# Staggering the two row halves of the PV matmuls, and a later first score step

## The chip, the cores and the metric

The kernel runs on one core of a Trainium2 chip. Times are device microseconds (us) of one execution. The engines have short names in the profile: PE is TensorE (matmuls), PEld its weight loads, DVE is VectorE, ACT is ScalarE, POOL is GpSimd, SP is SyncE, which here only issues DMAs. ACTq and SPq are the DMA-issuing instructions of ACT and SP.

## What is computed

A transformer block of which attention and feed-forward part work on the same normalised input: 2048 tokens of 576 features, 32 heads of 18 features each, a sliding window of 256 tokens, and a gated feed-forward layer with 4608 hidden features. All in bfloat16.

```python
def _A_ref(x, wqkv, wo):
    B, S, D = x.shape
    H = 32; Dh = D // H; W = 256
    q, k, v = split_into_heads(x @ wqkv)
    scores = jnp.einsum("bhqd,bhkd->bhqk", q, k) * (Dh ** -0.5)
    mask = (idx[:, None] - idx[None, :] >= 0) & (idx[:, None] - idx[None, :] < W)
    p = _softmax(jnp.where(mask[None, None], scores, -1e9), axis=-1)
    o = jnp.einsum("bhqk,bhkd->bhqd", p, v)
    return merge_heads(o) @ wo

def _B_ref(x, w1, w3, w2):
    h = _silu(jnp.einsum("bsd,df->bsf", x, w1)) * jnp.einsum("bsd,df->bsf", x, w3)
    return jnp.einsum("bsf,fd->bsd", h, w2)

xn = _layernorm(x)
return x + _A_ref(xn, A_wqkv, A_wo) + _B_ref(xn, B_w1, B_w3, B_w2)
```

## The kernel before

The 2048 tokens are worked in four chunks of 512 (`c` = 0 to 3). Each chunk has three phases on TensorE: the projections to q, k and v (line 437), gate/up (line 668), and the down projection with the output projection of attention (lines 719 and 725). The program is written as one list of operations (`add`); each goes to its engine in the order of the list, and `resolve` (line 90) puts in the semaphore waits that the buffers' readers and writers call for. An engine, ACT's and SP's DMA issues included, takes its instructions in this order, so one that waits holds those behind it.

**Gate/up** runs in 36 units (`u`). A unit is 9 pairs of matmuls (`unit_pairs`), each pair one matmul on the array's rows 0 to 63 and one on rows 64 to 127, both with 512 moving columns, into two PSUM banks, gate and up. Then `unit_tanh` (ACT, line 677) and two products in `unit_h` (DVE, lines 683 and 686) make 128 rows of `hT`. Three pairs of banks (`JOBS`) are taken in turn by units and by PV calls; two more (`SC`) belong to the scores.

**Attention** is put in between the units. The heads are worked in 8 groups of 4 (`G`), and a group's 512 queries in `NS` score steps (4 in the first chunk, 5 later; `steps_of`, line 547). A score step (`score_step`, line 882) is two to three pairs of matmuls into the two `SC` banks (line 561), one exp on ACT that reads both banks and writes a `pt` slot (line 570), and masks on POOL (line 597). The next score step can write the banks only when that exp is done.

When score steps come is planned by a clock that counts pairs of matmuls (`clock`; a slot in the text is one pair of gate/up). The first step comes when the clock reaches `start` (line 860): 20 in the first chunk, 46 in the others. After each step `spaced_step` (line 893) spreads the steps that are left over the room up to slot `last`, at least 7.5 slots apart, and a step that falls due within three slots after a unit's last pair is taken ahead of that pair.

At the end of units 2 and 3 of the first chunk, `span_main(2, G, "act", ...)` (line 965) issues DMAs that copy q and k of head groups 2 to 7 from `stage` into the layout of the scores: the two for q at unit 2, from ACT's queue (line 502 in `span_issue`), the three for k at unit 3, from SP's. `span_last` (line 967) sends further ones from SP at units 4 and 5. Groups 0 and 1 were copied before gate/up.

**PV** (`pv`, line 600) multiplies the exponentials with v, and there are four calls in each chunk, each for two head groups: three behind a unit of gate/up, at least `PV_AFTER` = 20 slots after their last score step, and the fourth in the down projection (line 995). A call goes through the key blocks of all score steps. For each key block it issues a wave of eight matmuls: two groups (`gi`), two pairs of heads (`pr`), and two row halves (`p`) of 64 keys each. Each matmul takes a 64 x 32 tile of the array (20 columns used): row half `p` and column strip `q = 2 * gi + pr`. All eight matmuls of a wave have the same number of moving columns, `nb * KB`, with `KB` = 64. Row half `p` adds up in its own bank, `banks[p]`. The key blocks of a call have, in units of 64 columns, widths 5, 3, 5, 2, 1, 5, 2, 5, 2 in the first chunk and 5, 3, 5, 3, 5, 2, 1, 5, 2, 1, 4, 4 in the others. The results are turned by DVE (`pv_out`, line 627), scaled, turned again and copied to `oT`, which the output projection reads at the end of the chunk.

The order before, in the loops of lines 610 to 614: wave by wave, in a wave strip by strip, and in a strip row half 0 and then row half 1.

Of the kernel before, what the change touches and what calls it, by code (L numbers as in the profile page):

```python
# [44 lines left out]
class _Prog:  # L45
# [13 lines left out]
    def add(self, eng, fn, r=(), w=(), j=(), dma=None, after=()):  # L59
        deps = []  # L60
        for k in r:
            deps += self.bufs[k].writers
        for k in w:
            g = self.bufs.get(k)
            if g is not None:
                deps += g.ahead(eng)
        for k in j:
            g = self.bufs[k].before
            if g is not None:
                deps += g.ahead(eng)  # L70
        op = _Op(eng, fn, deps + list(after), dma)
        op.after = tuple(after)
        self.n[eng] += 1
        op.pos = self.n[eng]
        if dma is not None:
            self.dma_count[dma] = self.dma_count.get(dma, 0) + 16
            op.cnt = self.dma_count[dma]
        for k in r:
            self.bufs[k].readers.append(op)
        for k in w:  # L80
            self.bufs[k] = _Gen([op], self.bufs.get(k))
        for k in j:
            self.bufs[k].writers.append(op)
        for k in w:
            if self.bufs[k].before is not None:
                self.bufs[k].before.before = None
        self.ops.append(op)
        return op
# [76 lines left out]
def bass_parallel_sum__sliding_block__glu_gated_swiglu__prompt_kernel(  # L165
# [24 lines left out]
    VW = 20  # L190
# [5 lines left out]
    add = P.add  # L196

    with ExitStack() as es:

        def sb(name, shape, dtype=dt.bfloat16):  # L200
            return es.enter_context(nc.sbuf_tensor(name, shape, dtype))

        NXP, NOF, NPT, NW13, NW2, NOD = 7, 4, 10, 3, 4, 2
        KB, NB, NV = 64, CH // 64, 12
# [20 lines left out]
        va = sb("va", [128, NV, G, 2, VW])  # L225
# [5 lines left out]
        def pt_slot(sl):  # L231
            kind, n = sl
            if kind == "pt":
                return pt[:, n, :, :]
            if kind == "sh":
                two = stage[:, 2 * n:2 * n + 2, :]
            else:
                two = hT[:, NF - 8 + 2 * n:NF - 6 + 2 * n, :]
            return two.rearrange("p t c -> p (t c)").rearrange("p (q r) -> p q r", r=2)

        def pt_keys(sl):
            kind, n = sl
            if kind == "pt":
                return [("pt", n)]
            if kind == "sh":
                return [("sh", 2 * n), ("sh", 2 * n + 1)]
            return [("h", NF - 8 + 2 * n), ("h", NF - 7 + 2 * n)]
# [16 lines left out]
        PS = es.enter_context(nc.psum_tensor("ps", [128, 8, 512], dt.float32))  # L264
# [6 lines left out]
        def ring():  # L271
            nonlocal ring_ctr
            i = ring_of[ring_ctr % 4]
            ring_ctr += 1
            return i

        def job():
            nonlocal job_ctr
            i = job_ctr % 3
            job_ctr += 1  # L280
            return JOBS[i]
# [263 lines left out]
        pt_of = {}  # L545

        def steps_of(c):

            if c == 0:
                return [[(0, 0, 5), (5, 5, 3)], [(1, 1, 5), (6, 6, 2), (7, 7, 1)],  # L550
                        [(2, 2, 5), (4, 4, 2)], [(3, 3, 5), (4, 6, 2)]]
            return [[(0, 0, 5), (-2, 0, 3)], [(1, 1, 5), (5, 5, 3)], [(2, 2, 5), (-3, 0, 2), (-4, 0, 1)],
                    [(3, 3, 5), (6, 6, 2), (7, 7, 1)], [(-1, 0, 4), (4, 4, 4)]]
# [45 lines left out]

        def pv(c, j, banks):  # L600

            seen = set()
            n_all = sum(len(st) for st in steps_of(c))
            n = 0
            for s, st in enumerate(steps_of(c)):
                col = 0
                for kb, q0, nb in st:
                    n += 1
                    pos = (c * NB + kb) % NV
                    for gi in range(2):  # L610
                        g = 2 * j + gi
                        sl = pt_of[(c, g, s)]
                        for pr in range(2):
                            for p in range(2):
                                first = (p, gi, pr) not in seen
                                seen.add((p, gi, pr))
                                q = 2 * gi + pr
                                add("pe", lambda e, p=p, q=q, pr=pr, sl=sl, g=g, pos=pos, q0=q0, nb=nb, col=col, first=first, n=n: e.matmul(  # L618
                                    PS[32 * q:32 * q + VW, banks[p], q0 * KB:(q0 + nb) * KB],
                                    va[64 * p:64 * p + 64, pos, g, pr, :],  # L620
                                    pt_slot(sl)[64 * p:64 * p + 64, col * KB:(col + nb) * KB, pr],
                                    start=first, stop=(n == n_all), tile_position=(64 * p, 32 * q), skip_group_check=True),
                                    r=pt_keys(sl) + [("va", pos)], **{"j" if any(k[0] == p for k in seen - {(p, gi, pr)}) or not first else "w": [("ps", banks[p])]})
                    col += nb

        def pv_out(b, i):
            add("dve", lambda e: e.transpose(uqs[i], PS[:, b, :]), r=[("ps", b)], w=uq_keys[i])
# [111 lines left out]
        for t in range(2):  # L739
# [3 lines left out]
            w=["wv"], dma="wv")  # L743
# [61 lines left out]
        for h in range(2):  # L805
# [9 lines left out]
            for n, (dst, src) in enumerate(moves):  # L815
                dealt.append(add("pool", lambda e, dst=dst, src=src: e.tensor_copy(dst, src),
                                 r=[f"wqk{h}", "wqkd"], **{"j" if n else "w": [f"wp{h}"]}))
# [32 lines left out]
        for c in range(NC):  # L850
# [6 lines left out]
            total = 9 * NF + len(att) + 3 * PV_COST  # L857
            if c:
                total += 9 * sum(COST[kind] for kind, _ in PROJ)
            start = 20 if c == 0 else 46  # L860
            last = total - 12
            nxt = soon = start
            clock = 0.0
# [55 lines left out]
            for u in range(NF):  # L919
# [18 lines left out]
                if next_pv in pv_ready and clock >= pv_ready[next_pv] and next_pv < 3:  # L938
                    j = next_pv
                    next_pv += 1  # L940
                    banks = job()
                    pv(c, j, banks)
                    clock += PV_COST
                    for g in (2 * j, 2 * j + 1):
                        for s in range(NS):
                            if pt_of[(c, g, s)][0] != "h":
                                free.append(pt_of[(c, g, s)])
                    later(u, lambda b=banks: (pv_out(b[0], 0), pv_out(b[1], 1), o_scale(0)))
                    later(u + 1, lambda j=j: (o_turn(2 * j, 0), o_turn(2 * j, 1), o_scale(1)))
                    later(u + 2, lambda j=j: o_turn(2 * j + 1, 0))  # L950
                    later(u + 3, lambda j=j: (o_turn(2 * j + 1, 1), o_pack(j, "sp")))
# [16 lines left out]
                if c == 0 and u == 13:  # L968
                    for t in range(4):
                        rows = A_wo[252 * (t // 2):252 * (t // 2) + 252, :].rearrange("(s p d) f -> p s d f", p=2, d=Dh)[t % 2, :, :, :]  # L970
                        add("sp", lambda e, t=t, rows=rows: e.dma_start(wo[0:126, t, :], rows),
                            r=["woz"], dma="wo", **{"j" if t else "w": ["wo"]})
# [13 lines left out]
            banks = ()  # L986
            for n, item in enumerate(p2_list(c)):
                p2_item(c, item, xs)
                if n == 3:
                    for u in sorted(side):  # L990
                        for what in side.pop(u):
                            what()
                elif n == 19:
                    banks = (ring(), ring())
                    pv(c, 3, banks)
                    pv_out(banks[0], 0)
                    pv_out(banks[1], 1)
                    o_scale(0)
                    o_turn(6, 0)
                    o_turn(6, 1)  # L1000
                    o_scale(1)
                    o_turn(7, 0)
                    o_turn(7, 1)
                    o_pack(3, "act")
                elif n == 40 and c + 1 < NC:
                    xn_send((c + 1) * TB + 3)
                elif n == 300 and c + 1 < NC:
                    xn_swap(c + 1, ("sp", "sp"))
                elif n in (100, 120) and c + 2 < NC:
                    t = (c + 2) * TB + (n == 120)  # L1010
                    xslot[t] = load_x(t)
# [31 lines left out]
```

## Time and profile before

| | |
|---|---|
| median of 3 runs | 564.29 us (563.03 to 564.5) |
| the profiled execution's own time | 562.96 us |
| its span (first to last instruction) | 561.3 us |
| granted TensorE clock, mean | 1.000 |
| PV matmuls (L618) | 1440 in 16 calls, 4% of the chain that ended last |
| score matmuls (L561) | 720, 6% of that chain |
| exps (L570) | 152, about 1.02 us each for 1024 elements |
| tanh of a unit (L677) | 144, 0.593 us each |

"Line" is the line of the kernel, so L618 is the matmul of PV. A matmul's length in a timeline includes its way through the array (376 ns for 512 columns), and matmuls overlap, so the distance between starts tells the rate. A busy share of 99% does not mean that no time is lost: what stands between one matmul's columns and the next one's start has to be read from the starts. The chain that ended last is followed back from the last instruction, each time to what released it.

### The profile page before, as it was taken

Reading aid. Unit: us, or ns where it says so; the run is one execution under the profiler, and the core shown is the slowest. Engines: PE = TensorE matmul, PEld = TensorE weight load, DVE = VectorE, ACT = ScalarE, POOL = GpSimd, SP = SyncE. Lnnn points to the kernel's source line nnn. Section 1 sums busy time; section 2 is a strip of 40 time slices with the busy share of each in tenths; the row PEclk is TensorE's granted clock in tenths of the full one; section 3 lists DMA queues with packets and bytes.
Section 4 is the critical chain, followed back from the end, with each engine's and each line's share of the span. In section 5 each row is a group of like instructions: output and inputs, shape, how many; then the busy total and the mean of one; then the engine's idle time right before and its main releaser. Section 6 shows DMA issues by size and latency. Waiting matters only on the chain.

```text
span 561.3 us, 15707 instructions
## 1 busy us (share of the span) xinstructions
PE 555.2 (99%) x6765; PEld 330.0 (59%) x6765; DVE 315.9 (56%) x586; ACT 253.3 (45%) x349; POOL 163.9 (29%) x384
## 2 busy tenths in 40 slices
PE   7999999999999999999999999999999999999998
PEld 3544544677655455477755545547776454555776
DVE  7666788710366778851046668884114567767211
ACT  3476666100286766600038677650004676666000
POOL 6433344400033445430003444533000333433000
PEclk9999999999999999999999999999999999999999
DMA  9986969965566477596546655969563674460552
GB/s 246 220 171 159 205 171 202 226 177 158 130 142 139 113 162 157 130 214 179 158 106 139 161 123 126 162 162 205 156 172 69 137 172 123 123 162 12 138 148 64
DMA packets 126565, 85.83 MB, mean 153 GB/s; under 512 B 33976, under 2 KB 124272, under 8 KB 126496
## 3 DMA queue, kind: packets, MB, share of 16 engines
q1 hardware_dynamic: 124469, 82.39, 63.0%
q10 hardware_dynamic: 2024, 2.43, 1.8%
q8 instruction: 53, 0.87, 0.7%
q14 instruction: 19, 0.13, 0.1%
HBM read 71.29 MB, written 2.36 MB: 131 GB/s over the span
## 4 chain that ended last, share of the span: by engine, by line
PE 97%; DMA 1%; DVE 1%; ACT 0%; ACTq 0%; POOL 0%; SPq 0%; issue 0%
PE ps L668 49%; PE ps L719 25%; PE ps L437 9%; PE ps L561 6%; PE ps L618 4%; PE ps L725 3%; DMA xp<-in_A_x_dram 1%; DVE xn L370 0%; ACT hT L570 0%; ACTq L502 0%; DVE stats L358 0%; DVE stats L360 0%; ACT xnT L389 0%; ACT th L677 0%; POOL rstd L364 0%
## 5 line engine op out<-in xcount | busy, mean ns | idle before, releaser
L668 PE MATMUL ps<-xnT,w 64*128 64x512 bf16 x1400 | 180.7, 376 | 0.0
L668 PE MATMUL ps<-xnS,w 64*128 64x512 bf16 x1120 | 151.6, 376 | 0.0
L719 PE MATMUL ps<-w,hT 128*128 128x288 bf16 x1152 | 147.1, 286 | 0.0
L683 DVE SCALAR_TENSOR_TENSOR gs<-th,ps 128x512 bf16<-128x512 bf16 x144 | 98.0, 680 | 79.6 <-ACT th L677 78.8
L570 ACT ACTIVATE pt<-ps 128x1024 bf16<-128x1024 f32 (+1 forms) x112 | 113.2, 1011 | 65.1 <-PE ps L561 64.6
L719 PEld LDWEIGHTS ps<-w,hT 128*128 128x128 bf16 x1152 | 112.1, 98 | 30.3 <-issue 1.7
L597 POOL TENSOR_TENSOR pt<-pt,mk 128x128 int32<-128x128 int32 (+1 forms) x199 | 80.8, 427 | 87.0 <-ACT pt L570 87.0
L686 DVE SCALAR_TENSOR_TENSOR hT<-gs,ps 128x512 bf16<-128x512 bf16 x144 | 98.9, 687 | 4.9
L668 PEld LDWEIGHTS ps<-xnT,w 64*128 64x128 bf16 x1400 | 64.9, 94 | 61.0 <-issue 0.3
L677 ACT ACTIVATE th<-ps 128x512 bf16<-128x512 f32 x144 | 85.4, 593 | 23.1 <-PE ps L668 22.8
L668 PEld LDWEIGHTS ps<-xnS,w 64*128 64x128 bf16 x1120 | 53.7, 94 | 57.0
L732 DVE TENSOR_TENSOR ofin<-ps,xp 128x288 bf16<-128x288 f32 x32 | 14.7, 458 | 119.7 <-PE ps L725 119.7
L450 ACT ACTIVATE stage<-ps 128x512 bf16<-128x512 f32 x16 | 9.6, 597 | 145.6 <-PE ps L437 143.2
L597 POOL TENSOR_TENSOR hT<-hT,mk 128x128 int32<-128x128 int32 (+1 forms) x31 | 12.4, 422 | 162.4 <-ACT hT L570 162.4
L561 PE MATMUL ps<-qv,kv 64*128 64x320 bf16 (+4 forms) x528 | 51.2, 260 | 0.1
L561 PEld LDWEIGHTS ps<-qv,kv 64*128 64x128 bf16 x528 | 25.3, 94 | 28.3 <-ACT pt L570 0.6
L437 PE MATMUL ps<-xnT,wp 64*128 64x512 bf16 (+1 forms) x360 | 38.3, 355 | 0.0
L570 ACT ACTIVATE stage<-ps 128x1024 bf16<-128x1024 f32 x24 | 24.6, 1024 | 12.6 <-PE ps L561 12.6
L640 DVE STREAM_TRANSPOSE od<-oq 128x256 bf16<-128x256 bf16 x64 | 25.8, 427 | 6.3 <-POOL oq L633 6.3
L437 PEld LDWEIGHTS ps<-xnT,wp 64*128 64x128 bf16 x360 | 17.4, 94 | 15.6 <-issue 0.7
L725 PE MATMUL ps<-wo,oT 128*128 128x288 bf16 x160 | 24.8, 286 | 0.0
L633 POOL TENSOR_TENSOR oq<-uq,rden 128x288 bf16<-128x288 f32 x16 | 10.8, 676 | 40.1 <-DVE rden L632 40.1
(58 smaller groups left out, 343.6 us busy)
## 6 DMA issues: line engine op xcount, KB each, us to landing
w<-in_B_w_dram SPq DMA_DIRECT2D x210, 192.0 KB, 4.2
w<-in_B_w_dram SPq DMA_DIRECT2D x72, 288.0 KB, 3.2
xp<-in_A_x_dram SPq DMA_DIRECT2D x28, 144.0 KB, 3.8
out_dram<-ofin SPq DMA_DIRECT2D x32, 72.0 KB, 2.1
xnS<-xnT SPq DMA_DIRECT2D x8, 256.0 KB, 4.8
oT<-od SPq DMA_DIRECT2D x48, 36.0 KB
pt<-in_A_wqkv_dram SPq DMA_DIRECT2D x4, 288.0 KB, 8.2
hT<-in_B_w_dram SPq DMA_DIRECT2D x6, 192.0 KB, 3.9
```

The costliest lines, as they stand in the source:

```text
L437: op = add("pe", lambda e, out_=out_, st=st, mv=mv, n=n, r0=r0, first=first: e.matmul(out_, st, mv, start=first, stop=(part == 1 and n == ...
L561: add("pe", lambda e, r0=r0, out_=out_, kb=kb, q0=q0, nb=nb: e.matmul(out_, kb4[r0:r0 + 64, g, kb + NV - NB, :] if kb < 0 else kv[r0:r0 + ...
L570: add("act", lambda e: e.activation(pt_slot(sl)[:, 0:w, :], PS[:, SC[0]:SC[1] + 1, 0:w].rearrange("p r q -> p q r"), ACT.Exp, scale=scale) ...
L597: add("pool", lambda e, vb=vb, mm=mm: e.tensor_tensor(vb, vb, mm, ALU.mult), r=(key if n == 0 else []) + ["mk"], **{"w" if n == 0 else "j" ...
L618: add("pe", lambda e, p=p, q=q, pr=pr, sl=sl, g=g, pos=pos, q0=q0, nb=nb, col=col, first=first, n=n: e.matmul(PS[32 * q:32 * q + VW, banks ...
L640: add("dve", lambda e: e.transpose(od[i][:, g % 2, c0:c0 + CH // 2], oq[:, c0:c0 + CH // 2]), r=["oq", "oq0"], **{"j" if half or g % 2 els ...
L668: op = add("pe", lambda e, n=n, r0=r0, r=r, k=k, src=src: e.matmul(PS[:, b0 + r, :], wt[r0:r0 + 64, k, fl * 128:(fl + 1) * 128], src, star ...
L677: add("act", lambda e: e.activation(th[i][:], PS[:, bg, :], ACT.Tanh, scale=0.5), r=[("ps", bg)], w=[("th", i)])
L683: add("dve", lambda e: e.scalar_tensor_tensor(out=gs[i][:], in0=th[i][:], scalar=1.0, in1=PS[:, bg, :], op0=ALU.add, op1=ALU.mult), r=[("t ...
L686: add("dve", lambda e: e.scalar_tensor_tensor(out=hT[:, u, :], in0=gs[i][:], scalar=0.5, in1=PS[:, bu, :], op0=ALU.mult, op1=ALU.mult), r= ...
L719: add("pe", lambda e: e.matmul(bank, hT[:, f, tt * 128:(tt + 1) * 128], w2[sl][:, k, :], start=(f == 0), stop=False), r=[("h", f), ("w2", ...
L725: add("pe", lambda e: e.matmul(bank, oT[:, k, tt * 128:(tt + 1) * 128], wo[:, k, d0:d0 + HD], start=False, stop=(k == 4)), r=[("oT", j) fo ...
```

## The change

Two things are changed.

The first is the order of PV's matmuls. They are collected in waves for each row half, one wave being the four column strips of one key block. The loop then issues wave `i` of row half 0 and after it wave `i - 1` of row half 1. So half 0 runs one wave ahead; after its last wave there is one wave of half 1 alone. Operands, number of matmuls, accumulation banks and the start and stop marks of a half's own accumulation are the same.

The second is the planner's `start` in the first chunk: 28 in place of 20.

```diff
         def pv(c, j, banks):
-            seen = set()
-            n_all = sum(len(st) for st in steps_of(c))
-            n = 0
+            waves = [], []
             for s, st in enumerate(steps_of(c)):
                 col = 0
                 for kb, q0, nb in st:
-                    n += 1
-                    pos = (c * NB + kb) % NV
-                    for gi in range(2):
-                        g = 2 * j + gi
-                        sl = pt_of[(c, g, s)]
-                        for pr in range(2):
-                            for p in range(2):
...
+                    for p in range(2):
+                        waves[p].append((s, col, kb, q0, nb))
                     col += nb
+
+            def wave(p, i):
+                s, col, kb, q0, nb = waves[p][i]
+                pos = (c * NB + kb) % NV
+                for q in range(4):
+                    g, pr = 2 * j + q // 2, q % 2
+                    sl = pt_of[(c, g, s)]
+                    add("pe", lambda e, q=q, g=g, pr=pr, sl=sl: e.matmul(
+                        PS[32 * q:32 * q + VW, banks[p], q0 * KB:(q0 + nb) * KB],
+                        va[64 * p:64 * p + 64, pos, g, pr, :],
+                        pt_slot(sl)[64 * p:64 * p + 64, col * KB:(col + nb) * KB, pr],
+                        start=(i == 0), stop=(i == len(waves[p]) - 1), tile_position=(64 * p, 32 * q),
+                        skip_group_check=True),
+                        r=pt_keys(sl) + [("va", pos)], **{"j" if i or q else "w": [("ps", banks[p])]})
+
+            for i in range(len(waves[0]) + 1):
+                if i < len(waves[0]):
+                    wave(0, i)
+                if i:
+                    wave(1, i - 1)
...
-            start = 20 if c == 0 else 46
+            start = 28 if c == 0 else 46
```

More of the change, by code (lines that the diff above doesn't have):

```diff
@@ L607, in pv @@
                 for kb, q0, nb in st:
-                    n += 1
-                    pos = (c * NB + kb) % NV
-                    for gi in range(2):
-                        g = 2 * j + gi
-                        sl = pt_of[(c, g, s)]
-                        for pr in range(2):
-                            for p in range(2):
[L615 to L623, printed above, removed]
-                    col += nb
+                    for p in range(2):
+                        waves[p].append((s, col, kb, q0, nb))
+                    col += nb
+            def wave(p, i):
[16 more added lines that the diff above has]
+                    wave(1, i - 1)
         def pv_out(b, i):
```

## The prediction

> **What bounds the kernel.** I read the page first, then the chain of waits, then every gap between one matmul's columns and the next start, then the timelines of the two places that the change touches.
>
> ```profile
> span 561.3 us, 15707 instructions
> ...
> PE 555.2 (99%) x6765; PEld 330.0 (59%) x6765; DVE 315.9 (56%) x586; ACT 253.3 (45%) x349; POOL 163.9 (29%) x384
> ...
> PE 97%; DMA 1%; DVE 1%; ACT 0%; ACTq 0%; POOL 0%; SPq 0%; issue 0%
> PE ps L668 49%; PE ps L719 25%; PE ps L437 9%; PE ps L561 6%; PE ps L618 4%; PE ps L725 3%; DMA xp<-in_A_x_dram 1%; DVE xn L370 0%; ACT hT L570 0%; ACTq L502 0%; DVE stats L358 0%; DVE stats L360 0%; ACT xnT L389 0%; ACT th L677 0%; POOL rstd L364 0%
> ```
>
> The matmul engine sets the end. What it loses or saves moves the end by as much, since after the start-up (about 13 us) it waits for another engine at one place only, shown below. PV (L618) is 4% of the chain: 16 calls, four per chunk.
>
> The first PV in the matmul timeline (start, length, engine, line; each wave of 8 matmuls stands as a row of 4 for the first head group and a row of 4 for the second, left out where not needed):
>
> ```profile
> 48.64 0.38 PE L668 MATMUL ps<-xnT,w 64*128 64x512 bf16 x2
> ...
> 49.18 0.31 PE L618 MATMUL ps<-hT,va 64*20 64x320 bf16 x4
> 49.20 0.31 PE L618 MATMUL ps<-pt,va 64*20 64x320 bf16 x4
> 49.32 0.23 PE L618 MATMUL ps<-hT,va 64*20 64x128 bf16 x4
> 49.34 0.23 PE L618 MATMUL ps<-pt,va 64*20 64x128 bf16 x4
> 49.38 0.20 PE L618 MATMUL ps<-hT,va 64*20 64x64 bf16 x4
> 49.40 0.20 PE L618 MATMUL ps<-pt,va 64*20 64x64 bf16 x4
> 49.41 0.31 PE L618 MATMUL ps<-hT,va 64*20 64x320 bf16 x4
> ```
>
> The reader is to see that the eight matmuls of a wave start within about 25 ns and run side by side, and that the next wave starts as soon as the columns are through. By the records' start times, 320 columns take 0.141 to 0.143 us to the next wave, 192 take 0.085, 128 take 0.057, 64 take 0.028: 28.3 ns for 64 columns, against 27.0 in gate/up (512 columns, 0.2157 us). So little stands between waves. The weights of the next wave are already loading some 2 ns after the present wave's matmul of the same tile has started (LDWEIGHTS records).
>
> The place where the engine waits (the chain of waits from 26 to 34 us):
>
> ```profile
> 27.67 0.22 PE ps L561 x4
> 27.89 1.53 PE ps L668 x14
> 29.42 0.02 issue
> 29.44 0.60 ACT th L677
> 30.04 0.16 ACTq L502
> 30.19 0.04 issue
> 30.23 0.73 ACTq L502
> 30.97 0.05 issue
> 31.01 1.03 ACT hT L570
> 32.05 0.05 issue
> 32.09 0.36 PE ps L561 x4
> ```
>
> ACT issues two DMAs (q of head groups 2 to 7, L502) right behind the tanh of unit 2, from 29.45 to 30.97. The second score step (29.67) is done at 30.05, yet its exp starts at 31.01; the third score step needs the same two banks and starts at 32.09 where its turn was 31.83. That costs **0.26 us**.
>
> **Part 1, PV in two staggered rows.** Number and shape of the matmuls, their 96 (first chunk 72) weight loads, and the banks are unchanged; only the order changes, to four of row half 0 for wave i, then four of row half 1 for wave i-1. In 64-column units a call's waves are 5,3,5,2,1,5,2,5,2 in the first chunk (30) and 5,3,5,3,5,2,1,5,2,1,4,4 later (40). Now both halves have the same width at the same time. After, a wide wave of one half stands beside a narrow one of the other.
>
> I take matmuls to start in program order: in all nine waves of the first call the first group's four start before the second group's four. Then a matmul waits for its tile's last one, and all behind it wait too. By that rule the starts of row half 0 in a later chunk are 0,5,8,13,16,21,23,26,31,33,36,40 and those of half 1 are 5,10,13,18,21,26,28,31,36,38,40,44: the end is at **48 units, not 40**. Four of these eight are the last wave of half 1, run alone; four come where a wide wave of one half holds the narrow one queued behind it (half 0's wave 7 could start at 24 and starts at 26, behind half 1's wave 5). In the first chunk the same count ends at **37, not 30**.
>
> Calls before, from first start to the end of the last columns: 0.885 us mean in the first chunk, 1.2155 later (1.203 to 1.245). After, by 28.3 ns for a unit plus 0.007 (the first wave takes 0.148) and 0.012 (the starts of the last four): 37 x 0.0283 + 0.019 = 1.066, 48 x 0.0283 + 0.019 = 1.377. Added: 4 x 0.181 + 12 x 0.162 = **2.7 us**. If a half that runs alone streams as gate/up does, 27.0 ns throughout: 4 x 0.133 + 12 x 0.100 = 1.7. No row of before has the halves on different widths, so the other bounds are the rivals: 0 and below, or 6.2. I take 2.7, since PV's own rows are nearest. The 0.09 us before and 0.10 us after each call stay: tile shapes change there as before. DVE's transposes of the result (L627) start no earlier for the second bank; three of four calls have the following units to hide them, the fourth the whole of the down projection.
>
> The Trainium skill ("TensorE: Matmul & The Clock Gate", Part 3, The mechanism) says that matmuls keep program order in start and in end, and that a weight load runs beside a matmul only if it is for another row group. The first speaks against this change; strictly read (ends too) it gives the third rival's 571.1. The second would speak for it, but the trace disagrees: by it each wave of before would stand still for its loads, eight at the 8.3 ns spacing seen late in a call, or 67 ns; the seen excess is 2 to 9.
>
> **Part 2, first scores at slot 28 in place of 20.** By the planner's arithmetic, scores of the first chunk stood at unit.pair 2.2, 3.2, 4.2 ... 11.2, 12.0; after they stand at 3.1, 3.8, 4.8 ... 11.8, 12.1, and are the same from 12.8 on; PV calls stay at units 11, 18, 26. No instruction is added. But now the *first* exp falls behind ACT's two DMAs, and the second score step comes only 7 pairs later, not 9. Worked out: without a score step in unit 2 all is 0.216 earlier: tanh 2 at 29.22, the DMAs to 30.75, exp 0 from 30.80 to 31.82, second score step at 31.87 (0.05 from exp to score, as before). Its turn: unit 3 from 29.02, one pair, scores 0.218, seven pairs of 0.216, so 30.96. **Stall 0.91 where 0.26 was: +0.65 us.** Behind exp 0 on ACT stand exp 1 and tanh 3, so tanh 3 ends near 33.95 and DVE's two products (0.69 each) free unit 3's banks at 35.35; unit 6, which takes them next, begins near 36.6, so nothing more is late. The moved step is also past SP's k copies for groups 2 to 7; these are needed at the ninth step (10.2 before, 10.8 after) and gain margin. If a DMA issue took 0.60 or 0.83 (shortest and longest short ones on SP nearby) the part would cost 0.36 or 0.85. If the exp weren't held at all, the part gains the 0.26.
>
> **Sum.** 2.66 + 0.65 = 3.3 us. The profiled run took 562.96 (span 561.3, 1.7 around it), so its like would be 566.3; the median of the runs shown is 564.29, 1.3 above, so I forecast 564.29 + 3.3 = **567.6**, own range 566.3 to 568.1 (1.7 + 0.36 to 2.9 + 0.85). Runs of before spread 0.26%, so about 0.3% (1.7 us) is what can be told from no change.
>
> **Rivals.**
> *Row halves queue apart* (0.21). If a blocked matmul of one half doesn't hold the other's behind it, each half needs 40 (30) units, and part 1 costs nothing: 564.29 + 0.65 = 564.9. For it: the two halves write different banks and use different rows. Against: program order of starts in every wave; but before never has a free tile behind a blocked one, so it can't be excluded.
> *The weight loads are freed* (0.18), the other side. Late in a call loads come 8.3 ns apart (from 219.28 on in the call at 218.37 a 256-column wave starts its eight over 58 ns), and the narrow waves there are bound by them. If the stagger hides these, and the streaming excess too, calls fall to their bare columns (0.80 and 1.067): -4 x 0.085 - 12 x 0.148 = -2.1, and with part 2's loss 562.8; if part 2 gains instead, 561.9. It decides once a call saves more than 0.65 / 16 = 0.04 us. Against: until the 44th load of a call (the 60th in later chunks) none is late, and the excess over bare columns grows with width, which that of a load would not.
> *Full lockstep* (0.13). If a pair of half-waves lasts as long as its wider one, a later call needs 56 units and a first-chunk call 44: 12 x 0.388 + 4 x 0.379 = 6.2, in all 564.29 + 6.8 = 571.1.
>
> **Chances.** Forecast 0.48, rivals 0.21, 0.18, 0.13. Slower by over 0.3%: forecast nearly whole and lockstep, 0.60. Within: the first rival and 0.07 of the second, 0.28. Faster: 0.12. The range reaches from just under the second rival's 562.8 to 570.0; left out are most of lockstep and the far half of the second rival.
>
> **What would show it.** In the changed trace: a PV call of a later chunk 1.3 to 1.4 us from first to last columns, its last four matmuls alone for 0.11 us, and starts of half 1 held at the listed units (right); 1.2 or less refutes order-keeping, 1.6 means lockstep. Near 31 us a gap ahead of the second score step of 0.6 to 1.1 us, with ACT's DMA issue in its chain; no gap there refutes part 2. Gaps in gate/up elsewhere would mean a wait that I missed.

## The result

| | before | after |
|---|---|---|
| median | 563.99 us (12 runs, 562.44 to 564.75) | 565.69 us (12 runs, 564.68 to 566.11) |
| profiled execution, time and span | 562.96, 561.3 us | 565.31, 563.6 us |
| ratio | | 1.0029, 95% interval 1.002 to 1.0037 |

The change makes the kernel slower by 1.7 us (1.1 to 2.1 by the interval). The forecast was 3.3 us more, 567.6 us with a range from 566.3 to 568.1; the measured 565.69 us lies below that range.

The page of after shows the same picture as before: the matmul engine sets the end. PV is now line 616 and gate/up line 672.

```profile
span 563.6 us, 15707 instructions
...
PE 556.6 (99%) x6765; PEld 331.6 (59%) x6765; DVE 316.1 (56%) x586; ACT 252.5 (45%) x349; POOL 163.8 (29%) x384
...
PE 97%; DMA 1%; DVE 0%; ACTq 0%; ACT 0%; POOL 0%; issue 0%
```

So the difference has to be found in matmul starts. Two places hold it. The first is the place where ACT's two DMAs stand ahead of an exp; this is the chain of waits of after from 26 to 34 us (start, length, what):

```profile
25.88 3.26 PE ps L672 x30
29.13 0.02 issue
29.16 0.60 ACT th L681
29.75 0.15 ACTq L502
29.91 0.04 issue
29.95 0.73 ACTq L502
30.68 0.05 issue
30.73 1.03 ACT hT L570
31.76 0.05 issue
31.80 0.39 PE ps L561 x6
```

The chain runs from the tanh of unit 2 through both DMA issues and the *first* exp to the second score step at 31.80. Between the columns of the matmul before it and its start there are **0.910 us**. It is the only wait of that size behind the start-up; the 0.261 us of before, at the third score step, is gone.

The second place is PV. This is the first call in after's matmul timeline, some rows of it (widths 320, 192, 128 and 64 are the waves' columns, and a row names its first matmul's; `hT` is the first head group, `pt` the second):

```profile
49.53 0.31 PE L616 MATMUL ps<-hT,va 64*20 64x320 bf16 x2
49.54 0.31 PE L616 MATMUL ps<-pt,va 64*20 64x320 bf16 x2
49.56 0.32 PE L616 MATMUL ps<-hT,va 64*20 64x320 bf16 x2
49.56 0.31 PE L616 MATMUL ps<-pt,va 64*20 64x320 bf16 x2
49.68 0.25 PE L616 MATMUL ps<-hT,va 64*20 64x192 bf16 x2
49.68 0.25 PE L616 MATMUL ps<-pt,va 64*20 64x192 bf16 x2
49.71 0.24 PE L616 MATMUL ps<-hT,va 64*20 64x192 bf16 x2
...
50.00 0.30 PE L616 MATMUL ps<-pt,va 64*20 64x320 bf16 x1
50.01 0.19 PE L616 MATMUL ps<-pt,va 64*20 64x64 bf16 x2
50.12 0.31 PE L616 MATMUL ps<-hT,va 64*20 64x320 bf16 x3
...
50.33 0.31 PE L616 MATMUL ps<-hT,va 64*20 64x128 bf16 x3
...
50.47 0.22 PE L616 MATMUL ps<-hT,va 64*20 64x128 bf16 x2
50.49 0.22 PE L616 MATMUL ps<-pt,va 64*20 64x128 bf16 x2
```

In the program, half 0's wave of 192 columns stands *ahead* of half 1's wave of 320. In the trace half 1's 320 start at 49.56, 27 ns after half 0's, and half 0's 192 only at 49.68. So a blocked matmul of one half does not hold the other half's behind it. The weight loads pass each other too: the third load of half 0's third wave carries a semaphore wait, by which it can be told in the trace; it is the 15th load of the program and comes 19th, at 0.156 us of the call, after four loads of half 1 at 0.052 to 0.062. At the end of the call half 1 is a wave late all the same: its last 128 columns start at 50.47, alone.

Between these, the records of the weight loads show a pause. These are rows of the first call, the first three of before and the others of after (a row's length runs from its first load to the end of its last, so a row that spans the pause is longer):

```profile
49.40 0.11 PEld L618 LDWEIGHTS ps<-pt,va 64*20 64x20 bf16 x4
49.43 0.18 PEld L618 LDWEIGHTS ps<-hT,va 64*20 64x20 bf16 x4
49.54 0.11 PEld L618 LDWEIGHTS ps<-pt,va 64*20 64x20 bf16 x4
...
49.99 0.09 PEld L616 LDWEIGHTS ps<-pt,va 64*20 64x20 bf16 x2
50.01 0.17 PEld L616 LDWEIGHTS ps<-hT,va 64*20 64x20 bf16 x2
50.10 0.09 PEld L616 LDWEIGHTS ps<-pt,va 64*20 64x20 bf16 x2
50.12 0.09 PEld L616 LDWEIGHTS ps<-hT,va 64*20 64x20 bf16 x2
```

Up to 0.48 us after the call's first start (0.71 in later chunks) the next wave's loads follow each started matmul at once, but for the last few, which are already 8.3 ns apart. Then comes one gap of about 80 ns, and after it loads come 8.3 ns apart wherever no running wave holds them, in program order (the marked 55th of after's program stands 55th), to the end of the call. Before has the same pause at the same times, after its 49th (65th) load; after has it behind its 45th (61st). Half 0 streams a wave of 320 columns through the pause (from 0.46 us of this call). Half 1 is through with its 64 columns at 0.51, and its next loads stand behind the rest of half 0's: its wave of 320 starts at 0.59, where before's starts at 0.46. These 0.13 us are about what the call is longer by.

A PV call, first start to last columns, over 4 calls of the first chunk and 12 of the others:

| | first chunk | later chunks | all 16 calls |
|---|---|---|---|
| before | 0.885 us | 1.216 | 18.13 |
| after | 1.022 | 1.319 | 19.92 |
| the forecast's working | 1.066 | 1.377 | 20.79 |

That is +1.79 us for PV where 2.66 were forecast, and +0.65 us for the gap near 32 us, as forecast. Together 2.4, and the two profiled executions differ by 2.35. But the medians differ by 1.7 only. The experiments had to explain the PV cost and this missing 0.7.

### The profile page after: what moved, and what is told of

Same layout as the page of the kernel before. It is cut to its first block, busy times and chain, and to the rows that moved or that the text cites. A ratio compares the mean times of both kernels' runs of the same rounds, so it can differ in the third digit from the quotient of the medians.

```text
span 563.6 us, 15707 instructions
## 1 busy us (share of the span) xinstructions
PE 556.6 (99%) x6765; PEld 331.6 (59%) x6765; DVE 316.1 (56%) x586; ACT 252.5 (45%) x349; POOL 163.8 (29%) x384
## 4 chain that ended last, share of the span: by engine, by line
PE 97%; DMA 1%; DVE 0%; ACTq 0%; ACT 0%; POOL 0%; issue 0%
PE ps L672 49%; PE ps L723 25%; PE ps L437 9%; PE ps L561 6%; PE ps L616 4%; PE ps L729 3%; DMA xp<-in_A_x_dram 1%; DVE xn L370 0%; ACTq L749 0%; ACT hT L570 0%; ACTq L502 0%; ACT xnT L389 0%; ACT th L681 0%; POOL rstd L364 0%; DVE stats L358 0%
## 5 line engine op out<-in xcount | busy, mean ns | idle before, releaser
L616 PE MATMUL ps<-pt,va 64*20 64x320 bf16 (+4 forms) x1068 | 22.4, 254 | 0.0
```

The lines of the kernel that those rows point to most:

```text
L616: add("pe", lambda e, q=q, g=g, pr=pr, sl=sl: e.matmul(PS[32 * q:32 * q + VW, banks[p], q0 * KB:(q0 + nb) * KB], va[64 * p:64 * p + 64, po ...
```

## The experiments

Three theories of the stagger's cost were carried. **Order** is the forecast's: no matmul starts before one that is ahead of it. **Break**: the halves run free, but the pause finds half 1's next loads not issued yet, because half 0's stand ahead of them, and so half 1 falls late. **Tail**: half 1's last wave, alone at the end, is the cost, whatever comes before.

### The two parts alone

`stagger_only` is after with `start = 20`; `start28_only` is before with `start = 28`.

> The stagger with the first scores back at slot 20. Three theories of the stagger's cost. Order (the forecast's: no matmul starts before one ahead of it in the program): PV calls of 1.07 us in the first chunk and 1.38 later, +2.7 us in all. Break (the changed kernel's trace: the halves run free of each other until 0.48 us, later chunks 0.71, into a call; then loads pause for some 80 ns and after it arrive one pair per 8.3 ns in program order, which finds half 1 a wave behind): 1.02 and 1.32 us as in the changed kernel, +1.8 us. Tail (the last wave of half 1, 5 or 4 units of 27 ns, runs alone, whatever comes before): the same 1.02 and 1.32, +1.8 us. All: the gap near 32 us is again 0.26 us.

Measured: calls of 1.017 and 1.328 us, 1.88 more in all; the 0.261 us gap is back; ratio 1.0022 (1.0008 to 1.0035). Break and Tail have the size, Order hasn't. But there was another gap, of 1.634 us, ahead of the *first* score step, which before's profile doesn't have:

```profile
PE ps L561 <- DMA kv<-stage: 1.5, 1, 1.5
```

(the waits of the matmul engine in this run: who waited for what, us in total, times, longest). The first score step waited for the copy of k of head groups 0 and 1.

> PV in the old order, first scores at slot 28. If the first exp stands behind ACT's two DMA issues as in the changed kernel: one gap of 0.91 us ahead of the second score step near 31.8 us where before had 0.26, PV calls 0.885 and 1.216 us as before, +0.65 us in all (ratio 1.0012). If the gap in the changed kernel had to do with the stagger, none here and -0.26 us.

Measured: one gap of 0.906 us at the second score step, none at the first, calls 0.899 and 1.213 us, and a ratio of 0.9992 (0.9978 to 1.0006). The chain of this kernel:

```profile
28.49 0.60 ACT th L677
29.09 0.15 ACTq L502
29.24 0.04 issue
29.28 0.73 ACTq L502
30.02 0.05 issue
30.06 1.03 ACT hT L570
31.10 0.05 issue
31.14 0.39 PE ps L561 x6
```

So the gap has nothing to do with the stagger, and it is really lost in the trace, yet the median did not rise by 0.65 us (a ratio of 1.0012, outside the interval). Something else must be gained with slot 28.

### Grouping, and a lead given back early

`grouped_no_lead` issues four matmuls of half 0 and then four of half 1 of the *same* wave:

```diff
-            for i in range(len(waves[0]) + 1):
-                if i < len(waves[0]):
-                    wave(0, i)
-                if i:
-                    wave(1, i - 1)
+            for i in range(len(waves[0])):
+                wave(0, i)
+                wave(1, i)
```

> Four matmuls of row half 0, then the four of half 1 of the same wave: the new grouping without the lead, first scores at slot 20. Order, Break and Tail all expect calls within 0.02 us of 0.885 and 1.216, so no change (within 0.3 us). If the grouping by halves is what costs (four loads for one half in a row in place of alternate ones), calls are 1.02 and 1.32 as in the changed kernel.

Measured: 0.901 and 1.214 us, ratio 0.9993 (0.9977 to 1.0008). The grouping costs nothing that can be told. Here the first score step waited 0.623 us.

`lead_given_back`:

```diff
+            for i in range(len(waves[0])):
+                if i == 0:
+                    wave(0, 0)
+                if i < 3:
+                    wave(0, i + 1)
+                elif i > 3:
+                    wave(0, i)
+                wave(1, i)
```

> Half 0 leads by one wave through the first three waves only, then both halves issue the same wave; first scores at slot 20. Order: 35 units in place of 30 and 45 in place of 40 per call, so 1.01 and 1.30 us, +2.1 us or more. Break: the lead is gone before the pause, so 0.885 and 1.216 within 0.02, no change. Tail: no wave runs alone, no change.

Measured: 0.987 and 1.226 us, ratio 1.0011 (0.9995 to 1.0028). In the later chunks there is next to no cost, which excludes Order (1.30). In the first chunk 0.10 us were lost, which neither Break nor Tail had said. The load records tell why: the pause came at the same time as always (0.48 us) but after 45 loads, not 49, one load into half 1's wave of 320 columns, which then started at 0.56 in place of 0.46. That fits Break's mechanism, but I had not seen that the halves need not be a wave apart for it. It also shows that more than loads stand still in the pause: the matmul of that one load, begun at 0.484, started at 0.565, 4 ns ahead of the next load, and so in all four calls of the chunk.

### Where the lead counts

`lead_given_back_late` keeps the lead until well behind the pause and then lets half 1 catch up (`k` is the number of waves less 3); `lead_late` has no lead until two waves from the end.

```diff
+            for i in range(len(waves[0])):
+                k = len(waves[0]) - 3
+                if i == 0:
+                    wave(0, 0)
+                if i < k:
+                    wave(0, i + 1)
+                elif i > k:
+                    wave(0, i)
+                wave(1, i)
```

> Slot 20. Half 0 leads by one wave until well past the pause, then waits in the program until half 1 has caught up, so that the last two waves of a call are issued for both halves. Tail (the lone last wave is the cost): calls as before, 0.885 and 1.216 us, nothing lost. Break (the pause finds half 1's next loads not issued yet, and half 1 stays late to the end): 1.02 and 1.30 us, nearly the whole cost of the stagger.

```diff
+            for i in range(len(waves[0]) - 2):
+                wave(0, i)
+                wave(1, i)
+            for p in range(2):
+                for i in range(len(waves[0]) - 2, len(waves[0])):
+                    wave(p, i)
```

> Slot 20. Both halves issue the same wave until two waves from the end; then half 0's last two waves come ahead of half 1's last two. Tail: 5 and 4 units of 27 ns more, 1.02 and 1.32 us. Break: the pause finds the halves together, and half 1's last two waves are held only by the loads ahead of them at 8.3 ns a pair, four pairs or 33 ns: 0.92 and 1.25 us.

Measured: the lead given back late costs nearly everything, 1.020 and 1.310 us (ratio 1.0027, 1.0013 to 1.0041), though no wave is left alone at the end of the program's order: Break within 0.01, and Tail (0.885, 1.216) is out. A lead taken up only at the end costs 0.04 and 0.06 us (0.926 and 1.277; ratio 1.002, 1.0005 to 1.0034), where Break said 0.03 each and Tail 0.13 and 0.10. In the first chunk this is Break's; in the later ones it lies between the two, and what makes it there is not shown.

### The order of widths

Four kernels sort the waves of a call by width (`narrow_first`, `narrow_first_stagger`: narrow to wide; `wide_first`: wide to narrow), or mix them. The first three and `start30_only` (before with `start = 30`) have slot 30.

```diff
+            for w in waves:
+                w.sort(key=lambda x: x[4])
```

> Slot 30, old order of halves and strips, but the waves of a call sorted from narrow to wide. Narrow waves in mid-call (widths 2 and 1) use up loads faster than the 8.3 ns a pair at which they come late in a call; if that makes the pause at 0.48 (0.71) us, there is none here and calls are 30 and 40 units of 28.3 ns plus 0.02, 0.87 and 1.15 us (before 0.885 and 1.216), -0.8 us in all against slot 30 alone. If the pause has a fixed place in a call, it stays at 0.48 and 0.71 us; wide waves may cover it.

> The same, sorted from wide to narrow, slot 30. If loads at 8.3 ns a pair (67 ns for a wave) bind wherever narrow waves stand late in a call, the last four waves (2,2,2,1 or 2,2,1,1) take 67 ns each in place of 57 and 28: 0.93 and 1.25 us a call. If loads don't bind, 0.87 and 1.15.

> The stagger with the waves sorted from narrow to wide, slot 30. Tail: the last wave of half 1, 5 units wide, runs alone: 1.01 and 1.29 us a call. Break: without a pause in mid-call the halves stay free of each other to the end, so within 0.03 us of the narrow-first run's calls. Order (the forecast's): 35 and 45 units, also 1.01 and 1.29, but then the starts of half 1 are a full wave behind from the first wave on, where Tail and Break have the first waves together.

Measured: `narrow_first` 0.934 and 1.260 us (0.87 and 1.15 expected), so sorting makes PV *slower*: the pause comes already 0.13 to 0.16 us into the call, after 33 loads. That the narrow waves in front use up sooner what stood ready is a reading that fits, but it isn't shown. `wide_first` 0.929 and 1.245, as expected if loads of 8.3 ns bind wherever narrow waves stand late. `narrow_first_stagger` 0.988 and 1.288: 0.05 and 0.03 more than `narrow_first`. The ratios to before are 1.0017 (1.0004 to 1.0029), 1.0003 (0.9991 to 1.0015) and 1.0022 (1.0008 to 1.0037). The numbers that I had written don't part the theories, as their base had moved. The starts speak against Order: the first waves of both halves are 27 ns apart again.

`wide_first` sorts by `-x[4]`. `narrow_first` and `wide_first` keep before's order of halves and strips. `mixed_widths` puts a narrow wave between wide ones, in the kernel `q_copies_early` of the next section:

```diff
+            for w in waves:
+                w.sort(key=lambda x: -x[4])
+                half = (len(w) + 1) // 2
+                wide, narrow = w[:half], w[half:][::-1]
+                w[:] = [x for k in range(half) for x in (wide[k:k + 1] + narrow[k:k + 1])]
```

> q_copies_early with PV in the old order of halves and strips, but narrow waves always between wide ones (5,1,5,2,5,2,5,2,3 and 5,1,5,1,5,2,5,2,4,3,4,3). If narrow waves in a row use up the loads on hand and so make the pause: no pause in mid-call, calls of 0.87 and 1.15 us, 0.8 us less than q_copies_early. If the pause comes after a certain number of loads or a certain time in any order: still there near 0.5 or 0.7 us, calls as before within 0.03.

Measured: 0.885 and 1.194 us, 0.25 us less over 16 calls than `q_copies_early` (18.11 to 17.87). The slow pace wasn't avoided: after the 32nd load, at 0.20 us, none comes until 0.32 us, and from there they come 8.3 ns apart. The gap itself is no proof of a pause, since a wave of 320 columns that started at 0.18 us holds the next loads as long. But the slow pace came earlier than in before's order, so narrow waves in a row are not what makes it. By time 562.63 us against 563.40 of before, ratio 0.9984 (0.9967 to 1.0001): the fastest of all kernels run, but not clear of no change.

### What slot 28 gains

`before_again` is the kernel before:

> The kernel before once more, for a further profile with slot 20. If the first step's wait comes and goes: a gap there between 0 and 1.7 us, and all else as in the first profile. Calls of PV 0.885 and 1.216 us within 0.02.

It had the wait. This is the chain of its waits ahead of the first score step:

```profile
21.38 0.77 SPq L533
22.15 0.04 issue
22.19 6.07 DMA kv<-stage
28.26 0.05 issue
28.30 0.39 PE ps L561 x4
```

The last copy of k is issued by 22.2 us and lands 6.07 us later; the first score step starts at 28.30, with a gap of 1.752 us. Over the seven profiles of kernels with slot 20 and the copies in their old place, the gap at the first step was 0 (before), 1.75, 1.63, 0.62, 0, 0.91 and 0 us: mean 0.70. In the nine with slot 28 or later it was 0 each time. Slot 28 brings the first step behind the landing. That is the gain that stands against the loss of 0.65. Its size is rough, a mean of seven values, and the margin isn't always wide: from its issue the copy took 3.5 to 6.5 us to land over all profiles, and in `start30_only` it landed 0.05 us and in `mixed_widths` 0.13 us ahead of the first score step.

`k_copy_first` was to show this from the other side, with the copies issued ahead of four weight loads:

```diff
-                load_w13((), 4)
                 span_main(0, 2, "act")
+                load_w13((), 4)
```

> PV as before, slot 20; the q and k copies of head groups 0 and 1 are issued ahead of four weight loads in place of behind them, some 2.5 us earlier on SP's queue. If the landing of the k copy is what holds the first score step in some runs: no gap there, the second gap of 0.26 us near 32 us stays, and the median falls by the mean of the first gap in the four profiles with slot 20 (0, 1.63, 0.62, 0: 0.56 us, ratio 0.999). If the gap is there all the same, the copy is late for another reason.

It went the other way: ratio 1.0051 (1.0038 to 1.0064), a gap of 2.0 us at the first step. The edit moved the wrong copies. SP's queue in this kernel:

```profile
17.50 2.69 SPq L502 DMA_DIRECT2D kv<-stage  x3
20.23 2.67 SPq L323 DMA_DIRECT2D w<-in_B_w_dram  x4
22.95 1.68 SPq L533 DMA_DIRECT2D kv<-stage  x2
```

The copies that land last are those of L533, a little later in the program, and in the queue these now come right behind the four loads. The direction is right (k copies later, kernel slower), the expectation wrong. Why the landing takes longer in some runs stays open.

> PV as before, first scores at slot 30, which puts the second score step 9 pairs after the first again. In the stagger-only and grouped runs the first score step at slot 20 stood 1.63 and 0.62 us for the landing of the k copy; before's own profile had no such gap. If that wait comes and goes from run to run with slot 20 and not with a later slot: no gap at the first step, at most 0.1 us at the second (0.91 with slot 28, 0.26 with 20), so 0.2 us less span than before's profile and 0.5 to 1.2 us less by medians (ratio 0.998 to 0.999). If the first step's wait is not of that kind, the median falls by 0.2 us or less.

Measured: no gap at the first step nor at the second, as expected, but no gain either: 1.0008 (0.9991 to 1.0024). The profile shows where it went. Its chain near 49 us:

```profile
44.05 0.79 SPq L531
44.84 0.04 issue
44.88 3.24 DMA hT<-in_B_w_dram
48.12 1.03 issue
49.15 0.82 PE ps L668 x6
```

and its weight load:

```profile
49.12 0.36 PEld L668 LDWEIGHTS ps<-xnT,hT 64*128 64x128 bf16 x6 [1.70 <-DMA hT<-in_B_w_dram]
```

Unit 12 waits 1.39 us for its weights (the fourth weight buffer, which lies in `hT`). The chain names the first of two copies, landed at 48.12, and puts the rest down to "issue"; in the trace the second copy lands at 49.06, 0.06 us ahead of the load. Slot 30 moved the PV call that stood ahead of unit 12 behind it, and the weights came no earlier (49.06 here, 48.51 in before).

`q_copies_early` has slot 28 and issues ACT's two q copies at the end of unit 1:

```diff
-                if c == 0 and u in (2, 3):
-                    span_main(2, G, "act", slice(0, 2) if u == 2 else slice(2, None))
+                if c == 0 and u in (1, 3):
+                    span_main(2, G, "act", slice(0, 2) if u == 1 else slice(2, None))
...
-            start = 20 if c == 0 else 46
+            start = 28 if c == 0 else 46
```

> PV as before, slot 28, and ACT's two q copies for head groups 2 to 7 at the end of unit 1 in place of unit 2, so that they are through before the first exp. No gap at the first step and at most 0.1 us at the second, PV calls 0.885 and 1.216. If the first step's wait with slot 20 is worth its mean of 0.70 us over seven profiles: 0.70 + 0.26 less than before by medians, ratio 0.998. If it is worth nothing by medians: 0.26 less, ratio 0.9995. The weights of unit 12 may come in as the next wait, up to 0.5 us.

> The same with the stagger. Break: calls of 1.02 and 1.32, 1.8 us more than q_copies_early. The forecast's order-keeping: 1.07 and 1.38, 2.7 us more.

Measured: `q_copies_early` has no gap over 0.11 us behind the start-up at all, the shortest span of all (560.3 us), and 562.94 us by median against 563.40; but the ratio is 0.9997 (0.9978 to 1.0015), so a gain can't be told, and 0.998 is at the edge of the interval. The wait for unit 12's weights shows again in its two descendants, 0.61 us with the stagger and 0.92 with mixed widths (0.09 of each is the change of tile shape). With the stagger: calls 1.016 and 1.324, 1.84 us more in all. This is the stagger's price with both waits at the scores gone: Break's 1.8, not Order's 2.7. By time it is 564.69 us, 1.75 above `q_copies_early`, and the ratio to before 1.0019 (1.0004 to 1.0033); the intervals are too wide to part 1.8 from 2.7, so that rests on the calls.

## Why the prediction was wrong

**The direction and the main line held.** The matmul engine sets the end, the change costs, and both parts were costed at the right places. The size was 3.3 where 1.7 was measured, for two reasons, one in each part. In times, 567.6 was forecast and 565.69 measured: part 1 was 0.87 too dear, part 2 left out a gain of about 0.70, and 0.30 is the base (three runs of before gave 564.29, twelve 563.99). The low end of the range had part 1 at 1.7 already; what lies below it is the gain left out of part 2 and the base.

**Part 1: 2.66 forecast, 1.79 to 1.88 measured.** The step that failed is "a matmul waits for its tile's last one, and all behind it wait too". Half 1's first wave passes half 0's blocked second one by 0.12 us. Of the 8 units (7 in the first chunk) I had put 4 (2) down to such holding; those aren't there. The rest, 4 and 5 units, has the right size but another cause than the lone last wave that I named: `lead_given_back_late` has no lone wave and pays all the same. What is shown is that half 1 falls late at the pause in the loads, because its loads stand behind half 0's there. Some agreement was luck: the prediction named 1.3 to 1.4 us for a later call as a sign of being right, and it took 1.319; its lower price of 1.7 us (27.0 ns a unit) comes near too. Both were worked out from the same order rule, by which half 1's first wave starts at 5 units, 0.14 us; it started at 0.027. The evidence that I gave for order ("the first group's four start before the second group's four") was never a test, since no free tile stood behind a blocked one; I said so under the first rival, and should have given that rival more.

**The first rival** (halves apart) was right about how the halves run and wrong about the price, 0: it had no supply of loads in it. **The second** (loads freed) had the cause by the wrong end: loads do bind late in a call, and the stagger makes that worse. **Lockstep** is out with Order: it asked for 1.6 us a later call, and 1.32 was measured.

The Trainium skill ("TensorE: Matmul & The Clock Gate", Part 3, The mechanism) says that matmuls start and end in program order. The trace of after disagrees for matmuls of different row halves (27 ns against 0.15 us). The Trainium skill ("TensorE: Matmul & The Clock Gate", Part 1, Architectural detail) gives TensorE's queue a depth of 64. The pause after 33 loads in the narrow-first order and the slow pace after 32 in the mixed one (with their matmuls some 64 instructions) agree with that; the 49 and 65 of before's order don't by themselves.

**Part 2: the working held, its base did not.** The stall was forecast as 0.91 us and measured as 0.910 and 0.906; the PV calls stayed at their units. What failed is the sentence that after the start-up the engine "waits for another engine at one place only". That was true of one execution. The k copy's landing, 6.07 us after its issue in one run of the same kernel and 3.96 in another, put a wait of 0.70 us on average (0 to 1.75 in seven profiles) ahead of the first score step with slot 20, and slot 28 removes it. The sum had no term for this. So part 2 is worth 0.65 - 0.70, about nothing, and `start28_only` measured 0.9992 (0.9978 to 1.0006). With 1.8 for the stagger that gives the 1.7 of the result.

How exactly the wait at the first step counts by medians isn't settled: `start30_only` and `q_copies_early`, which lack it, gained less than its mean. The wait for unit 12's weights, which shows in profiles that reach unit 12 early (1.39, 0.18, 0.52, 0.61 and 0.92 us in five of the nine with slot 28 or later) and in none with slot 20, takes part of it back. What makes the pause in a PV call, and what sets its place, is open too; two narrow waves in a row are not it.

## What to carry to other kernels

A trace in which the parts of an array always work on equal widths says nothing of whether they hold each other up; before costing an uneven order by such a rule, take its opposite as nearly as likely. Where small matmuls run several to a wave, count their weight loads in program order: a reorder that puts one part's loads ahead of another's can make the other late where the loads come slowly, as here from the pause on. One profile shows one landing time for each DMA: an engine that "doesn't wait" for a copy with little margin waits in other runs, and the spread of the times shown (562.4 to 564.8 before, 564.7 to 566.1 after) is a hint of it.

## What the runs showed that was not expected

- Matmuls of the two row halves start out of program order: half 1's after 27 ns, though a blocked one of half 0 stood ahead and started at 149 ns. Weight loads pass each other in the same way until the pause, and keep program order after it.
- In a PV call weight loads of 20 columns pause once for some 80 ns, 0.48 us (0.71 in later chunks) into a call in the kernel's order, and then arrive every 8.3 ns where nothing else holds them; with narrow waves in front the pause comes at 0.13 to 0.16 us, after 33 loads. Sorting the waves made the calls 0.03 to 0.05 us longer than before's either way.
- The last k copy took 3.5 to 6.5 us to land, with weight loads issued before and after it on the same queue, and the wait for it differed by 1.75 us between two profiles of one kernel.
